# A decode step bound by its cache loads: K transposed in place, in a ring of eleven 16 KB units with a written-out plan of places

## The chip, the cores and the metric

The kernel runs on one core of a Trainium2 chip. A core has five engines that run their own instruction streams and meet at semaphores: PE (TensorE, matmuls), DVE (VectorE), ACT (ScalarE), POOL (GpSimd) and SP (SyncE, which here only issues transfers). Sixteen DMA engines move the data of all queues. The metric is the time of one execution in device microseconds (us); shown are the median of several runs and, for one profiled execution, its span from first to last instruction.

## What is computed

Two blocks work on the same four rows x (one token for each of four sequences, 1024 wide, bf16), and a gate mixes them.

```python
# A: attention of one new token against a cache; H = 32 heads, Dh = 128, Sk = 8192
q = (x @ wq).reshape(B, 1, H, Dh).transpose(0, 2, 1, 3)
scores = einsum("bhqd,bhkd->bhqk", q, k_cache) * Dh ** -0.5
p = softmax(scores)
o = einsum("bhqk,bhkd->bhqd", p, v_cache)
a = o.transpose(0, 2, 1, 3).reshape(B, 1, H * Dh) @ wo
# B: a gated MLP, F = 3584, added to x with a sigmoid weight r = x @ w_r
b = x + (silu(x @ w_gate) * (x @ w_up)) @ w_down * sigmoid(r)
# the mix
g = sigmoid((x * gate_w).sum(-1))
out = g * a + (1 - g) * b
```

Nearly all of the data is the two caches: each has 4 x 32 x 8192 x 128 bf16 values, 268 MB; the five weight matrices add some 39 MB. Every byte is used for one token only, so the work is a stream of some 576 MB through the core.

## The kernel before

**Tiles.** A *pair* is the K (or V) cache of four heads of one sequence: 8.39 MB, 64 KB in each of 128 partitions (`kv_view`). 128 heads make ND = 32 K pairs and 32 V pairs, called K0 to K31 and V0 to V31 here. A partition holds 256 consecutive positions of one head, 128 values each; 32 partitions make a head. A pair is worked in RD = 4 quarters of 16 KB per partition.

**The ring.** All large loads go through one SBUF tile of NS = 5 slots of 32 KB per partition. `load_pair` (line 189) takes the next two slots in turn. If they lie next to each other, one transfer brings the pair (line 196); where the ring wraps, and for V pairs called with `apart`, two transfers bring one half each (line 200). V29 to V31 are cut further by lines 568 to 573. `wd_piece` takes two slots for w_down, and `wo_block` puts four 8 KB blocks of wo into each of two slots. Every transfer is issued by SP in program order, and each waits, at SP, until what it overwrites has been read.

**A K pair** (`k_pair`, line 476 on for `spread`, 494 and 499 for the work). Scores need K with its 128 values on the partitions, and it arrives with positions there. DVE transposes blocks of 32 x 32 four-byte words: for each quarter two transposes (the two halves of the 128 values), eight in a pair, each from the ring into one of three buffers TB (`turned`, 8 KB per partition). PE then runs eight matmuls on each transposed half, with the heads' queries, spread out in Z, as stationary weights, and adds to the scores of the group in PSUM (S_ps). So a ring slot of K is free once DVE has read it, and a TB buffer once PE has.

**A V pair** (`v_pair`, line 579). PE takes V from the ring as it came: 64 matmuls with the probabilities PB as weights, into o_ps. A V slot is free once PE has read it. After every second V pair `sum_up` adds the four parts of o_ps: one step on ACT (L605), and three on DVE (L609), which wait in a list and are put into the next K pair after its third transpose; `finish` and `scaled` (L625, L634, L637) follow in the same K pair.

**Order.** Groups of GD = 8 K pairs share one softmax; after the eighth pair of a group its maximum, exponentials and their transposition run on DVE and ACT. PE, DVE and POOL run in the order of the program text. That order is: wq, w_gate, K0, K1, w_up, K2 to K7, then K8, V0, K9, V1 and so on (V follows K by LAG = 8), then w_down, V24 to V31, and the wo blocks, of which the first two are loaded ahead of V31.

Of the kernel before, what the change touches and what calls it, by code (L numbers as in the profile page):

```python
# [8 lines left out]
BF = mybir.dt.bfloat16  # L9
F32 = mybir.dt.float32  # L10
U32 = mybir.dt.uint32
# [101 lines left out]
def kernel(  # L113
# [15 lines left out]
    nc = tc.nc  # L129
    P = 128  # L130
    Bn, Sq, D = A_x.shape
    _, H, Sk, Dh = A_k_cache.shape
    F = B_w_gate.shape[1]
    DT = D // P
# [3 lines left out]
    CJ = 64  # L138
    JT = JR // CJ
    RD = 2 * JT  # L140
    GD = QP // RD
    GH = GD * NQ
    ND = Bn * H // NQ
# [5 lines left out]
    FR = 4  # L149
    FG = F // (P * FR)  # L150
    NB = 512
    NH = D // NB
    RING = JR * Dh
    NS = 5
    assert Sq == 1 and Dh == P and D % P == 0 and F % (P * FR) == 0
    assert H % GH == 0 and JR == 128 and RD * GD == QP and D % NB == 0
    scale = float(Dh) ** -0.5
# [3 lines left out]
    const = ctx.enter_context(tc.tile_pool(name="const", bufs=1))  # L161
# [7 lines left out]
    nc.at_finalize(drop_implied)  # L169
    nc.at_finalize(begin_early)  # L170

    ring = const.tile([P, NS, RING], BF, name="ring")
    turn = [0]


    TB = [const.tile([P, CJ * Dh // 2], BF, name=f"TB{i}") for i in range(3)]
    tb_turn = [0]

    def turned(rows, n, dtype=BF):
        t = TB[tb_turn[0] % 3]  # L180
        tb_turn[0] += 1
        return t[0:rows, 0:n] if dtype == BF else t[0:rows, 0:2 * n].bitcast(dtype)

    def slots(n):
        at = turn[0]
        turn[0] = (at + n) % NS
        return at

    flat = ring[:].rearrange("p s n -> p (s n)")

    def load_pair(src, n, apart=False):

        a = slots(2)
        if a + 1 < NS and not apart:
            lo = a * RING
            nc.sync.dma_start(out=flat[:, lo:lo + 2 * n], in_=src)
            return [flat[:, lo:lo + n], flat[:, lo + n:lo + 2 * n]]
        halves = [ring[:, a], ring[:, (a + 1) % NS]]
        for i, half in enumerate(halves):
            nc.sync.dma_start(out=half[:, 0:n], in_=src[:, i * n:(i + 1) * n])  # L200
        return halves


    S0 = scp.tile([P, 4, NB], F32, name="S_ps")
# [8 lines left out]
        return b[:, 0:n].rearrange("p (%s) -> p %s" % (" ".join(names), " ".join(names)), **dict(zip(names, shape)))  # L213

    N = H * Dh
    wq_at = load_pair(A_wq.rearrange("(c t) n -> c (t n)", t=DT), DT // 2 * N)
    NX = Bn + 2
    x6 = const.tile([NX, D], BF)
    nc.sync.dma_start(out=x6[0:Bn], in_=x2)
# [10 lines left out]
    n = 1  # L230
# [19 lines left out]
    for half in range(2):  # L250
        for e in range(2):
            nc.gpsimd.tensor_copy(out=R[:, 2 * half + e].rearrange("p (n j) -> p n j", n=4),
                                  in_=ident[:, 64 * half + e:64 * half + 64:2].unsqueeze(1).to_broadcast([P, 4, 32]))
# [57 lines left out]
    TW = DT // 2  # L311


    FI = FG * FR - 1
    FB = P * FI
    SX = 5
# [37 lines left out]

    def gu_piece(view, w_i):

        ws = load_pair(view.rearrange("(c t) f -> c (t f)", t=DT), TW * F)

        def cols(w, t, i):
            row = w[:, t * F:t * F + FB].rearrange("p (f m) -> p f m", m=FI)  # L360
            if i < FG - 1:
                return [(0, FR, row[:, :, FR * i:FR * i + FR])]
            return [(0, FR - 1, row[:, :, FR * i:FI]), (FR - 1, FR, w[:, t * F + FB:(t + 1) * F])]
        x_rows(o_ps[w_i], ws, FG, cols)
# [28 lines left out]
        nc.vector.tensor_tensor(out=hS[:], in0=hs_ps[0:72], in1=cS[:], op=ALU.mult)  # L393

    def wd_piece():
        a = slots(2)
        assert a + 1 < NS and (FI + SX) * D == 2 * RING
        w = flat[:, a * RING:(a + 2) * RING]
        at = FI * D
        nc.sync.dma_start(out=w[:, 0:at], in_=wdv)  # L400
        for u in range(2):
            nc.sync.dma_start(out=w[32 * u:32 * u + 12, at:at + SX * D], in_=wd_apart[u])
        nc.sync.dma_start(out=w[64:72, at:at + D], in_=wd_rest)
        parts = [(hT[:, i // FR, i % FR, :], w[:, i * D:(i + 1) * D]) for i in range(FI)]
        parts += [(hS[:, v, :], w[0:72, at + v * D:at + (v + 1) * D]) for v in range(SX)]
        for i, (lhsT, rows) in enumerate(parts):
            for n in range(NH):
                mm_acc(n, lhsT, rows[:, n * NB:(n + 1) * NB], start=(i == 0))
# [11 lines left out]
                                 rhs=OT[:, WB * g0 + k:WB * g1:WB, :], start=True, stop=True, skip_group_check=True)  # L420
        nc.vector.tensor_copy(out=LT[:, :, g0:g1, :], in_=lp)  # L421

    wo_home = {}

    def wo_block(g, r0=0, r1=FR, half=None):

        home, at = divmod(g, 4)
        if home not in wo_home:
            wo_home[home] = ring[:, slots(1)].rearrange("p (g r n) -> p g r n", g=4, r=FR)
        w = wo_home[home][:, at]  # L430
        if half is None:
            nc.sync.dma_start(out=w[:, r0:r1].rearrange("p r n -> p (r n)"),
                              in_=wov[:, g, r0:r1].rearrange("p r n -> p (r n)"))
        else:
            nc.sync.dma_start(out=w[:, r0, half * NB:(half + 1) * NB], in_=wov[:, g, r0, half * NB:(half + 1) * NB])

        def use():
            for r in range(r0, r1):
                for n in range(NH) if half is None else [half]:
                    mm_acc(n, LT[:, r, g, :], w[:, r, n * NB:(n + 1) * NB])  # L440
        return use
# [25 lines left out]
    def kv_view(cache, d):  # L467
        b, h0 = heads(d)
        return cache[b, h0:h0 + NQ].rearrange("h (r j) d -> (h r) (j d)", j=2 * JR)
# [8 lines left out]
    def k_pair(d):  # L478
        g, t = divmod(d, GD)
        Z = Zt[d % 2]  # L480
        if d == 0:
            spread(0)
        if t == 0:
            S_ps[g] = S0
        sps = S_ps[g]
        ks = load_pair(kv_view(A_k_cache, d), RING)
        for n in range(RD):
            kn = ks[n // JT].rearrange("p (c j h m) -> p c h j m", c=JT, h=2, m=Dh // 2)[:, n % JT]
            s = QP - 1 - (RD * t + n)
            for half in range(2):  # L490
                step = 2 * n + half
                flat_t = turned(P, CJ * Dh // 2)
                T = flat_t.rearrange("p (j i e) -> p j i e", j=CJ, e=2)
                nc.vector.transpose(out=flat_t.bitcast(U32).rearrange("p (j i) -> p j i", j=CJ), in_=kn[:, half].bitcast(U32))  # L494
                if step < 2 and ahead:
                    ahead.pop(0)()
                for e in range(2):
                    for z in range(4):
                        nc.tensor.matmul(sps[:, z, :], lhsT=Z[:, 2 * half + e, s:s + P], rhs=T[:, 16 * z:16 * z + 16, :, e],  # L499
                                         start=(t + n + half + e == 0),  # L500
                                         stop=(t == GD - 1 and n == RD - 1 and half + e == 2))
                if step == 2:
                    flush_sums()
                if step == RD and d + 1 < ND:
                    spread(d + 1)
                if step == RD:
                    flush()
                if step == RD + 2:
                    flush_late()
        if t == GD - 1:  # L510
            ahead.extend(softmax(g))
            while g > 0 and ahead:
                ahead.pop(0)()
# [45 lines left out]
    def v_pair(d):  # L559
        b, h0 = heads(d)  # L560
        g, t = divmod(d, GD)
        tv = t % GV
        row = NM * tv
        flush_sums()
        vv = kv_view(A_v_cache, d)
        if d < ND - 3:
            vs = load_pair(vv, RING, apart=d >= ND - GD + 2)
        else:
            vs = [ring[:, slots(1)] for _ in range(2)]
            for half, cuts in ((0, 1), (1, 2)) if d < ND - 1 else ((0, 2), (1, 4)):  # L570
                for c in range(cuts):
                    lo, hi = c * RING // cuts, (c + 1) * RING // cuts
                    nc.sync.dma_start(out=vs[half][:, lo:hi], in_=vv[:, half * RING + lo:half * RING + hi])
        for u in range(4 * RD):
            n, z = divmod(u, 4)
            vn = vs[n // JT]
            for w in range(4):
                j0 = CJ * (n % JT) + 16 * z + 4 * w
                nc.tensor.matmul(o_ps[w // 2][row:row + NM, w % 2, :],  # L579
                                 lhsT=PB[:, RD * (d % NW) + n, z].rearrange("p w s j -> p (w s j)"),  # L580
                                 rhs=vn[:, j0 * Dh:(j0 + 4) * Dh], start=(u == 0), stop=(u == 4 * RD - 1),
                                 skip_group_check=True)
            if u == 1:
                flush()
            if u == 7:
                flush_late()
        if tv == GV - 1:
            sum_up(d, g, t, b, h0)

        if g == NG - 1:  # L590
            if t < 2:
                spread_p(d + NW)
            if t == 3:
                spread_p(d + NW - 1, 2)
        elif t == NW - 1:
            spread_p(d + 1, NW)
        elif t == GD - 1:
            if g + 1 < NG - 1:
                spread_p(d + 1, NW)
            else:  # L600
                spread_p(d + NW)
# [47 lines left out]
    order = []  # L649
# [69 lines left out]
```

## Time and profile before

| | before |
|---|---|
| time, median of 3 runs | 1342.75 us (1342.62 to 1343.24) |
| profiled execution, span | 1340.5 us |
| PE busy | 1067.9 us, 80% |
| DVE busy | 638.3 us, 48% |
| queue of the loads (q1) | 575.69 MB, 99.7% of 16 engines' span |
| mean rate | 430 GB/s |

The page tells each engine's busy time, then cuts the span into 40 equal slices, each with the busy share of every engine in tenths and the rate of the transfers. The costliest groups follow: source line, engine, operation, what it writes and reads, how often, busy time and the mean of one, and then how long the engine was idle just before such instructions and what ended that. A group's mean is the time from issue to end of one, and PE's matmuls overlap, so the distance from one to the next is shorter than that mean. Further answers of the trace give the waits by engine and line (total, number, longest), the timeline of single instructions, and the chain of work that ended last, where a row "DMA" runs from a transfer's issue to its landing, the time in the queue included.

### The profile page before, as it was taken

To read this page: it belongs to the slowest core of one execution; us is meant where nothing else is said; L and a number is where in the kernel's file an instruction comes from. 1 tells how busy PE (TensorE), PEld (TensorE's weight loads), DVE (VectorE), ACT (ScalarE), POOL (GpSimd) and SP (SyncE) were. 2 spreads that over 40 slices of the span, in tenths; PEclk is the share of its full clock that TensorE was granted. 3 is DMA by queue.
4 is the path that set the end of the run, shared out by engine and by line. 5 is a ranking of instruction groups with operands and counts; after the bars stand their busy time and mean duration, and the time that the engine had idled before them with its cause. 6 is when DMAs were issued, how large, how long until landed. Compare 5 with 4: busy or idle time off the path is not lost.

```text
span 1340.5 us, 6937 instructions
## 1 busy us (share of the span) xinstructions
PE 1067.9 (80%) x4654; PEld 141.3 (11%) x1422; DVE 638.3 (48%) x385; ACT 57.7 (4%) x58; POOL 66.6 (5%) x174
## 2 busy tenths in 40 slices
PE   2666878887778788777879778789697879889888
PEld 0101000001011010101001010101011011111111
DVE  2555988556544347554436256646145555100001
ACT  0000000100010000100010000100000000110000
POOL 2000000100010000100010000100001000100000
PEclk9787999898998998898989888899898889889889
DMA  9999999999999999999999999999999999999998
GB/s 415 433 436 435 437 436 424 438 430 430 435 437 426 439 431 428 433 438 431 434 433 433 436 433 438 419 434 431 438 433 441 426 423 435 438 425 430 429 425 348
DMA packets 15512, 576.14 MB, mean 430 GB/s; under 512 B 1740, under 2 KB 2004, under 8 KB 3170
## 3 DMA queue, kind: packets, MB, share of 16 engines
q1 hardware_dynamic: 15474, 575.69, 99.7%
q8 instruction: 24, 0.39, 0.1%
q14 instruction: 6, 0.05, 0.0%
q10 hardware_dynamic: 8, 0.00, 0.0%
HBM read 575.68 MB, written 0.01 MB: 429 GB/s over the span
## 4 chain that ended last, share of the span: by engine, by line
DMA 62%; DVE 22%; PE 13%; another core or an unknown queue 1%; issue 0%; ACT 0%; SPq 0%; DVEq 0%
DMA ring<-in_A_k_cache_dram 51%; DVE TB L494 20%; DMA ring<-in_A_v_cache_dram 9%; PE o_ps L579 8%; PE S_ps L499 2%; PE acc L287 2%; DVE OS L609 2%; DMA x<-in_gate_w_dram 2%; DVE mx L521 0%; PE o_ps L333 0%; PE S_ps L333 0%; PE led L625 0%; DVE PT L535 0%; ACT TB L530 0%
## 5 line engine op out<-in xcount | busy, mean ns | idle before, releaser
L494 DVE STREAM_TRANSPOSE TB<-ring 128x2048 uint32<-128x2048 uint32 x256 | 568.2, 2278 | 471.7 <-DMA ring<-in_A_k_cache_dram 463.9
L499 PE MATMUL S_ps<-TB,Z 128*128 128x512 bf16 x2048 | 531.5, 414 | 186.0 <-DVE TB L494 178.4
L579 PE MATMUL o_ps<-ring,PB 128*64 128x512 bf16 x2048 | 468.5, 392 | 44.9 <-DMA ring<-in_A_v_cache_dram 43.7
L499 PEld LDWEIGHTS <-Z 128*128 128x128 bf16 x512 | 53.0, 103 | 649.6 <-issue 649.6
L579 PEld LDWEIGHTS <-PB 128*64 128x64 bf16 x512 | 57.6, 112 | 447.8 <-issue 443.4
L617 DVE SCALAR_TENSOR_TENSOR OS<-o_ps,mE,OS 128x512 f32<-128x512 f32 x5 | 3.8, 751 | 134.9 <-ACT OS L615 134.9
L476 POOL COPY Z<-qa 32x4 bf16<-32x4 bf16 x128 | 25.6, 200 | 719.2 <-PE S_ps L499 693.2
L555 POOL COPY PB<-PT 32x1024 bf16<-32x1024 bf16 (+3 forms) x23 | 33.3, 1446 | 456.8 <-PE o_ps L579 350.7
L605 ACT ACTIVATE OS<-o_ps,mE 128x512 f32<-128x512 f32 x11 | 7.6, 687 | 673.6 <-PE o_ps L579 673.6
L553 ACT COPY PB<-PT 32x1024 bf16<-32x1024 bf16 (+3 forms) x21 | 30.3, 1443 | 22.3 <-PE o_ps L579 17.3
L609 DVE SCALAR_TENSOR_TENSOR OS<-o_ps,mE,OS 128x512 f32<-128x512 f32 x33 | 24.3, 737 | 1.5
L530 ACT ACTIVATE TB<-S_ps,mx 128x2048 bf16<-128x2048 f32 x4 | 7.9, 1967 | 321.9 <-DVE mx L527 321.9
L287 PE MATMUL acc<-ring,hT 128*4 128x512 bf16 x54 | 14.7, 444 | 5.4 <-ACT TB L530 5.4
L245 PE MATMUL S_ps<-identb,x 6*128 6x6 bf16 x8 | 0.6, 196 | 22.6 <-DMA x<-in_gate_w_dram 22.6
L333 PE MATMUL o_ps<-ring,xw 128*4 128x512 bf16 (+2 forms) x128 | 13.2, 499 | 4.8 <-DMA ring<-in_B_w_gate_dram 4.8
L287 PE MATMUL acc<-ring,LT 128*4 128x512 bf16 x64 | 14.7, 379 | 0.4 <-DVE LT L421 0.4
L625 PEld LDWEIGHTS o_ps<-selg,OS 128*128 128x128 f32 x88 | 11.5, 191 | 9.3 <-issue 8.8
L535 DVE STREAM_TRANSPOSE PT<-TB 128x2048 bf16<-128x2048 bf16 x4 | 9.2, 2312 | 6.4 <-ACT TB L530 6.4
L521 DVE TENSOR_REDUCE mx<-S_ps 128x1 f32<-128x2048 f32 x4 | 9.1, 2282 | 6.2 <-PE S_ps L499 6.2
L625 PE MATMUL o_ps<-selg,OS 128*128 128x8 f32 x88 | 10.5, 245 | 0.0
L637 DVE SCALAR_TENSOR_TENSOR OT<-led,sgb,rinv 128x8 bf16<-128x8 f32 x5 | 1.2, 237 | 18.2 <-PE led L625 18.2
L615 ACT ACTIVATE OS<-o_ps,mE 128x512 f32<-128x512 f32 x5 | 3.4, 687 | 147.9 <-PE o_ps L579 147.9
(83 smaller groups left out, 89.2 us busy)
## 6 DMA issues: line engine op xcount, KB each, us to landing
ring<-in_A_v_cache_dram SPq DMA_DIRECT2D x18, 4096.0 KB, 28.9
ring<-in_A_k_cache_dram SPq DMA_DIRECT2D x14, 4096.0 KB, 33.2
ring<-in_A_v_cache_dram SPq DMA_DIRECT2D x6, 2048.0 KB, 36.7
ring<-in_B_w_gate_dram SPq DMA_DIRECT2D x1, 7168.0 KB
ring<-in_B_w_up_dram SPq DMA_DIRECT2D x1, 7168.0 KB, 37.1
ring<-in_B_w_down_dram SPq DMA_DIRECT2D x1, 6912.0 KB
ring<-in_A_wo_dram SPq DMA_DIRECT2D x4, 1024.0 KB, 32.5
ring<-in_A_v_cache_dram SPq DMA_DIRECT2D x4, 1024.0 KB, 36.0
```

The lines of the kernel that those rows point to most:

```text
L287: nc.tensor.matmul(acc(n), lhsT=lhsT, rhs=rhs, start=start, stop=True, skip_group_check=True)
L333: nc.tensor.matmul(ps[32 * k:32 * k + Bn, z, :].rearrange("p (f r) -> p f r", r=FR)[:, :, lo:hi], lhsT=xT[TW * half + t], rhs=rhs, start=( ...
L476: nc.gpsimd.tensor_copy(out=Z[at, :, QP - 1 + QP * q], in_=qa[at, :, h0 + q, b])
L494: nc.vector.transpose(out=flat_t.bitcast(U32).rearrange("p (j i) -> p j i", j=CJ), in_=kn[:, half].bitcast(U32))
L499: nc.tensor.matmul(sps[:, z, :], lhsT=Z[:, 2 * half + e, s:s + P], rhs=T[:, 16 * z:16 * z + 16, :, e], start=(t + n + half + e == 0), stop ...
L521: nc.vector.tensor_reduce(out=mx[:, 0:1], in_=sps[:].rearrange("p z n -> p (z n)"), axis=AX.X, op=ALU.max)
L535: nc.vector.transpose(out=PT[:].rearrange("p j i -> p (j i)"), in_=PTs)
L553: nc.scalar.copy(out=Bv[at, :, :, q, :], in_=Pv[at])
L555: nc.gpsimd.tensor_copy(out=Bv[at, :, :, q, :], in_=Pv[at])
L579: nc.tensor.matmul(o_ps[w // 2][row:row + NM, w % 2, :], lhsT=PB[:, RD * (d % NW) + n, z].rearrange("p w s j -> p (w s j)"), rhs=vn[:, j0 ...
L609: nc.vector.scalar_tensor_tensor(out=OS[:], in0=o_ps[w // 2][:, w % 2, :], scalar=mE[:, w:w + 1], in1=OS[:], op0=ALU.mult, op1=ALU.add)
L625: nc.tensor.matmul(oT, lhsT=OS[:, q * Dh:(q + 1) * Dh], rhs=selg[:, q].rearrange("p t s -> p (t s)"), start=(q == 0), stop=(q == 3), skip_ ...
```

## The change

K is transposed in place: input and output of the DVE transpose are the same elements of the ring, so that the TB buffers no longer carry K. They shrink from three of 8 KB to two of 4 KB, and the ring grows from 160 to 176 KB per partition: NU = 11 units of UN = 16 KB. A pair takes four units. Instead of taking turns, each load takes its place from a list, `plan`, of 68 entries in load order: the first unit, and whether the pair's quarters are worked upward or downward. A pair at unit 9 takes 9, 10, 0, 1, in two transfers. `wo_places` lists where the eight wo blocks go, in steps of 8 KB. V26 to V29 come in one transfer each; V30 in one half and two quarters, V31 in two and four parts (`cuts`).

The K matmuls read the transposed words where they lie: for 16 positions 32 elements with step 2 each, in place of 512 elements with step 2 in one run.

```diff
-    NS = 5
+    UN = RING // 2
+    NU = 11
-    ring = const.tile([P, NS, RING], BF, name="ring")
-    TB = [const.tile([P, CJ * Dh // 2], BF, name=f"TB{i}") for i in range(3)]
+    flat = const.tile([P, NU * UN], BF, name="ring")
+    UP, DOWN = False, True
+    plan = iter([
+        (4, UP), (0, UP), (4, UP), (0, DOWN), (7, UP), (3, UP), (7, UP), (1, UP), (5, DOWN), (0, DOWN), (7, UP), (1, UP),
+        (5, UP), (9, UP), (2, UP), (7, UP), (1, UP), (5, UP), (0, DOWN), (7, UP), (1, UP), (5, DOWN), (0, DOWN), (7, UP),
+        (1, UP), (5, DOWN), (0, DOWN), (7, UP), (3, UP), (7, UP), (1, UP), (5, DOWN), (0, DOWN), (7, UP), (1, UP), (5, DOWN),
+        (0, DOWN), (7, UP), (3, UP), (7, UP), (1, UP), (5, DOWN), (0, DOWN), (7, UP), (1, UP), (5, DOWN), (0, DOWN), (7, UP),
+        (2, UP), (7, UP), (0, UP), (5, UP), (9, UP), (2, UP), (7, UP), (0, UP), (5, UP), (9, UP),
+        (3, UP), (7, UP), (1, UP), (5, DOWN), (0, DOWN), (7, UP), (2, UP), (6, UP), (0, UP), (4, UP)])
+    wo_places = [20, 21, 16, 17, 18, 19, 0, 1]
+    TB = [const.tile([P, 4 * NB], BF, name=f"TB{i}") for i in range(2)]
-    def load_pair(src, n, apart=False):
-        a = slots(2)
-        if a + 1 < NS and not apart:
-            lo = a * RING
+    def load_pair(src, n, cuts=(1, 1)):
+        place, down = next(plan)
+        lo = place * UN
+        at = [lo, lo + n] if place + 4 <= NU else [lo, 0]
+        halves = [flat[:, x:x + n] for x in at]
+        if cuts == (1, 1) and at[1]:
             nc.sync.dma_start(out=flat[:, lo:lo + 2 * n], in_=src)
+        else:
+            for i, half in enumerate(halves):
+                step = n // cuts[i]
+                for x in range(0, n, step):
+                    nc.sync.dma_start(out=half[:, x:x + step], in_=src[:, i * n + x:i * n + x + step])
+        return halves, list(range(RD))[::-1] if down else list(range(RD))
...
-        ks = load_pair(kv_view(A_k_cache, d), RING)
-        for n in range(RD):
-            kn = ks[n // JT].rearrange("p (c j h m) -> p c h j m", c=JT, h=2, m=Dh // 2)[:, n % JT]
+        ks, order = load_pair(kv_view(A_k_cache, d), RING)
+        for k, n in enumerate(order):
+            unit = ks[n // JT][:, (n % JT) * UN:(n % JT + 1) * UN]
+            kn = unit.bitcast(U32).rearrange("p (j h i) -> p h j i", j=CJ, h=2)
+            T = unit.rearrange("p (j h i e) -> p h j i e", j=CJ, h=2, e=2)
-                flat_t = turned(P, CJ * Dh // 2)
-                T = flat_t.rearrange("p (j i e) -> p j i e", j=CJ, e=2)
-                nc.vector.transpose(out=flat_t.bitcast(U32).rearrange("p (j i) -> p j i", j=CJ), in_=kn[:, half].bitcast(U32))
+                nc.vector.transpose(out=kn[:, half], in_=kn[:, half])
-                        nc.tensor.matmul(sps[:, z, :], lhsT=Z[:, 2 * half + e, s:s + P], rhs=T[:, 16 * z:16 * z + 16, :, e],
+                        nc.tensor.matmul(sps[:, z, :], lhsT=Z[:, 2 * half + e, s:s + P], rhs=T[:, half, 16 * z:16 * z + 16, :, e],
...
-        if d < ND - 3:
-            vs = load_pair(vv, RING, apart=d >= ND - GD + 2)
-        else:
-            vs = [ring[:, slots(1)] for _ in range(2)]
-            for half, cuts in ((0, 1), (1, 2)) if d < ND - 1 else ((0, 2), (1, 4)):
+        vs, order = load_pair(vv, RING, {ND - 2: (1, 2), ND - 1: (2, 4)}.get(d, (1, 1)))
         for u in range(4 * RD):
-            n, z = divmod(u, 4)
+            n, z = order[u // 4], u % 4
```

The number of transposes, matmuls and bytes is the same. With all work of a K quarter done in the ring, a ring place of K is overwritten only after PE's matmuls on it.

More of the change, by code (lines that the diff above doesn't have):

```diff
@@ L170 @@
     nc.at_finalize(begin_early)
-    ring = const.tile([P, NS, RING], BF, name="ring")
-    turn = [0]
-    TB = [const.tile([P, CJ * Dh // 2], BF, name=f"TB{i}") for i in range(3)]
+    flat = const.tile([P, NU * UN], BF, name="ring")
[7 more added lines that the diff above has]
+        (3, UP), (7, UP), (1, UP), (5, DOWN), (0, DOWN), (7, UP), (2, UP), (6, UP), (0, UP), (4, UP)])
@@ L177 @@
+    wo_places = [20, 21, 16, 17, 18, 19, 0, 1]
+    TB = [const.tile([P, 4 * NB], BF, name=f"TB{i}") for i in range(2)]
     tb_turn = [0]
     def turned(rows, n, dtype=BF):
-        t = TB[tb_turn[0] % 3]
+        t = TB[tb_turn[0] % 2]
         tb_turn[0] += 1
         return t[0:rows, 0:n] if dtype == BF else t[0:rows, 0:2 * n].bitcast(dtype)
[L184 to L189, printed above, removed]
-    def load_pair(src, n, apart=False):
-        a = slots(2)
-        if a + 1 < NS and not apart:
-            lo = a * RING
[L196 to L201, printed above, removed]
+    def load_pair(src, n, cuts=(1, 1)):
+        place, down = next(plan)
+        lo = place * UN
+        at = [lo, lo + n] if place + 4 <= NU else [lo, 0]
+        assert at[1] or (n == RING and lo + n == NU * UN and not down)
+        halves = [flat[:, x:x + n] for x in at]
+        if cuts == (1, 1) and at[1]:
+            nc.sync.dma_start(out=flat[:, lo:lo + 2 * n], in_=src)
+        else:
[4 more added lines that the diff above has]
+        return halves, list(range(RD))[::-1] if down else list(range(RD))
@@ L215 @@
     N = H * Dh
-    wq_at = load_pair(A_wq.rearrange("(c t) n -> c (t n)", t=DT), DT // 2 * N)
+    wq_at, _ = load_pair(A_wq.rearrange("(c t) n -> c (t n)", t=DT), DT // 2 * N)
     NX = Bn + 2
@@ L355, in gu_piece @@
     def gu_piece(view, w_i):
-        ws = load_pair(view.rearrange("(c t) f -> c (t f)", t=DT), TW * F)
+        ws, _ = load_pair(view.rearrange("(c t) f -> c (t f)", t=DT), TW * F)
         def cols(w, t, i):
@@ L395, in wd_piece @@
     def wd_piece():
-        a = slots(2)
-        assert a + 1 < NS and (FI + SX) * D == 2 * RING
-        w = flat[:, a * RING:(a + 2) * RING]
+        lo = next(plan)[0] * UN
+        assert (FI + SX) * D == 2 * RING and lo + 2 * RING <= NU * UN
+        w = flat[:, lo:lo + 2 * RING]
         at = FI * D
@@ L421, in o_rows @@
         nc.vector.tensor_copy(out=LT[:, :, g0:g1, :], in_=lp)
-    wo_home = {}
     def wo_block(g, r0=0, r1=FR, half=None):
[L427 to L430, printed above, removed]
+        at = wo_places[g] * FR * D
+        w = flat[:, at:at + FR * D].rearrange("p (r n) -> p r n", r=FR)
         if half is None:
@@ L485, in k_pair @@
         sps = S_ps[g]
-        ks = load_pair(kv_view(A_k_cache, d), RING)
-        for n in range(RD):
-            kn = ks[n // JT].rearrange("p (c j h m) -> p c h j m", c=JT, h=2, m=Dh // 2)[:, n % JT]
+        ks, order = load_pair(kv_view(A_k_cache, d), RING)
[3 more added lines that the diff above has]
+            T = unit.rearrange("p (j h i e) -> p h j i e", j=CJ, h=2, e=2)
             s = QP - 1 - (RD * t + n)
             for half in range(2):
-                step = 2 * n + half
-                flat_t = turned(P, CJ * Dh // 2)
-                T = flat_t.rearrange("p (j i e) -> p j i e", j=CJ, e=2)
-                nc.vector.transpose(out=flat_t.bitcast(U32).rearrange("p (j i) -> p j i", j=CJ), in_=kn[:, half].bitcast(U32))
+                step = 2 * k + half
+                nc.vector.transpose(out=kn[:, half], in_=kn[:, half])
                 if step < 2 and ahead:
@@ L498, in k_pair @@
                     for z in range(4):
-                        nc.tensor.matmul(sps[:, z, :], lhsT=Z[:, 2 * half + e, s:s + P], rhs=T[:, 16 * z:16 * z + 16, :, e],
-                                         start=(t + n + half + e == 0),
-                                         stop=(t == GD - 1 and n == RD - 1 and half + e == 2))
+                        nc.tensor.matmul(sps[:, z, :], lhsT=Z[:, 2 * half + e, s:s + P], rhs=T[:, half, 16 * z:16 * z + 16, :, e],
+                                         start=(t + k + half + e == 0),
+                                         stop=(t == GD - 1 and k == RD - 1 and half + e == 2))
                 if step == 2:
@@ L565, in v_pair @@
         vv = kv_view(A_v_cache, d)
-        if d < ND - 3:
-            vs = load_pair(vv, RING, apart=d >= ND - GD + 2)
-        else:
-            vs = [ring[:, slots(1)] for _ in range(2)]
-            for half, cuts in ((0, 1), (1, 2)) if d < ND - 1 else ((0, 2), (1, 4)):
-                for c in range(cuts):
-                    lo, hi = c * RING // cuts, (c + 1) * RING // cuts
-                    nc.sync.dma_start(out=vs[half][:, lo:hi], in_=vv[:, half * RING + lo:half * RING + hi])
+        vs, order = load_pair(vv, RING, {ND - 2: (1, 2), ND - 1: (2, 4)}.get(d, (1, 1)))
         for u in range(4 * RD):
-            n, z = divmod(u, 4)
+            n, z = order[u // 4], u % 4
             vn = vs[n // JT]
```

## The prediction

> **What bounds the kernel now.** I read the page's slices and queues first, because they say whether the stream of loads ever stops; then the costliest groups, the waits of SP's own queue, and last the timeline and the chain around single K pairs. From the page:
>
> ```profile
> DMA  9999999999999999999999999999999999999998
> GB/s 415 433 436 435 437 436 424 438 430 430 435 437 426 439 431 428 433 438 431 434 433 433 436 433 438 419 434 431 438 433 441 426 423 435 438 425 430 429 425 348
> ...
> q1 hardware_dynamic: 15474, 575.69, 99.7%
> ...
> L494 DVE STREAM_TRANSPOSE TB<-ring 128x2048 uint32<-128x2048 uint32 x256 | 568.2, 2278 | 471.7 <-DMA ring<-in_A_k_cache_dram 463.9
> L499 PE MATMUL S_ps<-TB,Z 128*128 128x512 bf16 x2048 | 531.5, 414 | 186.0 <-DVE TB L494 178.4
> L579 PE MATMUL o_ps<-ring,PB 128*64 128x512 bf16 x2048 | 468.5, 392 | 44.9 <-DMA ring<-in_A_v_cache_dram 43.7
> ```
>
> The one queue that carries the caches has work in all 40 slices: 575.69 MB at about 432 GB/s is the whole span. DVE and PE wait for K, PE for V. The kernel can get faster only if the bytes move faster, and gets slower as soon as the queue runs empty. How far is it from empty? The waits of SP's queue, which issues the loads:
>
> ```profile
> SPq L196 <- DVE TB L494: 458.6, 25, 28.8
> SPq L196 <- PE o_ps L579: 370.3, 19, 27.3
> ```
>
> A load is issued when the ring place it overwrites has been read: a K place by the DVE transposes (L494), a V place by PE (L579). A K pair between sums, then one that holds them (timeline, then the chain):
>
> ```profile
> 270.23 17.66 DVE L494 STREAM_TRANSPOSE TB<-ring 128x2048 uint32<-128x2048 uint32 x8 [15.63 <-DMA ring<-in_A_k_cache_dram]
> ...
> 279.15 0.33 SPq L196 DMA_DIRECT2D ring<-in_A_k_cache_dram  x1
> ...
> 287.94 1.96 PE L499 MATMUL S_ps<-TB,Z 128*128 128x512 bf16 x8 [0.23 <-DVE TB L494]
> ...
> 289.97 0.95 POOL L476 COPY Z<-qa 32x4 bf16<-32x4 bf16 x4 [32.34 <-PE S_ps L499]
> ```
>
> ```profile
> 434.03 29.79 DMA ring<-in_A_k_cache_dram
> ...
> 463.91 6.70 DVE TB L494 x3
> 470.61 0.64 DVE OS L609
> ...
> 472.13 0.75 DVE OS L609
> 472.88 8.80 DVE TB L494 x4
> ...
> 481.80 2.22 DVE TB L494
> ...
> 484.06 1.96 PE S_ps L499 x8
> ```
>
> The pair that landed at 270.14 (issued 245.86, 24.28 to landing) is transposed in eight steps of 2.21 us; half of its ring place was free at 279.15, and PE had finished its last eight matmuls by 289.97 (POOL's copy waits for just that). So from landing to the end of PE's reading: 19.83 us. With the three sums of L609 inside, 463.82 to 486.0: 22.2 us; in the pair that landed at 308.83, where a reciprocal is added, PE ends at 331.43: 22.6 us.
>
> What does a load cost? Streaming, the chain has K landings at 581.43 (544.25 + 37.18) and 620.13 (590.44 + 29.69): 38.70 us for a K and a V pair, 19.35 each. Into an empty queue there is one row, the first load of the program, equally large:
>
> ```profile
> ring<-in_A_wq_dram SPq DMA_DIRECT2D x1, 21.9
> ```
>
> **The change part by part.**
>
> *Fewer, larger transfers.* The page counts 32 transfers of 4096 KB (14 K, 18 V) and 6 of 2048 KB; of the new plan's pairs only K9, V20 and K31 wrap, and only V30 and V31 are cut: 7 and 4. In the packet records a 64 KB packet takes 2425 ns, two of 32 KB 2435, four of 16 KB 2515. 25 transfers of 128 packets less make 1600 pairs of packets by 9.6 ns over 16 engines: 0.96 us. V29's second half saves (256 x 629 - 64 x 2425) ns / 16 = 0.36 us. Together -1.3 us, all on the path, since the queue is the path.
>
> *Transposing in place.* 256 transposes stay, 128x64x32 with a strided output in place of a dense one, and the matmuls read runs of 32 with step 2 in place of one run of 512. No row has an in-place one. The nearest, PT (L535, 2312 ns, dense, 2-byte) and L494 itself (2278 ns, 2.21 apart), are 1.5% apart; I take 2.21. Nothing excludes a cheaper one; the dearer side is bounded loosely by a tenth (2.43). DVE no longer waits for a TB buffer (7.7 us of waits in all): worth nothing, because the eight steps already run back to back in 17.66 us. The matmuls keep 1.96 us a step, under DVE's 2.21, with 0.25 us of cover.
>
> *A K place is now held until PE has read it*, not until DVE has: 2.0 us later for every K pair. Most issues can bear it. In the plan's regular stretch (K at 7, V at 1, K at 5 downward, V at 0 downward) a K load needs half of the K pair two transfers back: free 4 x 2.21 + 2.1 = 10.9 us after that pair's landing (13.2 with sums). A V load needs three quarters of the V pair two back, which PE starts at 19.9 and reads in 13.93: free at 30.3, wanted at 38. The queue then holds work for 19.0 us after a landing (19.35 less the 0.35 us from last byte to semaphore), so 5 to 8 us are spare.
>
> *Five issues have no such room.* Going through the 68 places in load order, five loads overwrite the *last-read* quarter of the K pair two transfers back, so need all of it: up (places 7 to 10) after K0 (4 to 7); K12 (7 to 10) after K11 (5 to 8 read upward); K17 after K16, K22 after K21 and K27 after K26 (7 to 10 after 7 to 10). Between them lies one transfer of 19.35 us; the pair takes 19.83 us. The queue empties every time. SP waits, the next V issue queued behind in order (its own place comes free 10 us later, so it loses nothing), and DVE and PE then wait for the late K pair. Each costs read-out + lone load - two streamed loads: 19.83 + 21.9 - 38.70 = 3.0 us for K0, K11, K21 (no sums: V pairs before them are even or absent), 22.2 + 21.9 - 38.7 = 5.4 for K16 and 22.6 + 21.9 - 38.7 = 5.8 for K26, which follow V7 and V17. Sum 9.0 + 11.2 = 20.2 us. If restarting cost nothing (19.35 for 21.9), 0.5, 3.0 and 3.4: 7.9 us. I take 21.9, the same size into an empty queue. The Trainium skill's page "DMA: Bandwidth & Descriptors" (Anatomy of one DMA) gives a fixed cost of some 2.0 us per transfer, mostly completion, next to bytes over 436 GB/s: as an estimate 21.2 us alone, and 16.7 us for the five together; no run here shows that figure, and its fit is for another issuing path. It speaks against letting the queue run dry as the wq row does.
>
> *Levelling.* In the semaphore records the sixteen engines finish one transfer 1.6 us apart at 60 us and 4.8 at the end: engine after engine loses about 1.4 us now and then and never regains it. An empty queue waits for the slowest, so each stretch between the five spells can lose its own 1.4 instead of sharing three: 0 to +4.4 us; I take 1.0, since spells also hide such losses.
>
> *V26 to V29 whole, the tail.* V29 now starts on PE only when all of it has landed. From that landing PE owes V29 13.9, V30 13.9 + 1.8 (L625), o_rows and wo block 0 2.6, V31 13.9 and, from 1323.8 to its end at 1337.45, the other wo blocks with finish, 13.6: 59.8 us, against 59.7 from V29's last landing (1277.7) to PE's end before. So PE has no idle time left there, where it had 3.9 us before 1287.6; any wait adds. I take 0.3, between 0 and 1. The ring of eleven units itself gives no time; wo blocks in fixed places overwrite pairs long read.
>
> Sum: -1.3 + 20.2 + 1.0 + 0.3 = +20.2 us. The profiled execution has a span of 1340.5 us, 2.2 under the median of 1342.75; the span becomes 1360.7 and the time about 1363.0.
>
> **The rivals.**
> *Dry spells nearly free.* The queue empties, but a restart costs only what is missing: 7.9 - 1.3 + 0.3 = +6.9, 1350 us. For it: the wq load was the program's first, colder than any later one (its first packets took 3.2 us, later ones 2.4). Against it: one landing and one issue lie in each spell anyway.
> *In-place transposes dearer.* Strided writes into lines that PE reads next to them could take 2.43 us: five spells x 8 x 0.22 = +8.8, 1372 us; above 2.5 us the K-only start would go dry too, over 1376. Nothing in the profile has this form, and DVE's input already is strided the same way.
> *Not slower.* In-place transposes at 1.8 us or less: read-out 16.6 us, so that even a restart is covered in three spells; or sums moved by waits out of the pair. Then -1.3 + 0.3, 1341.8 us, or 2 to 3 us less if the engines end level. The deciding point is a transpose of 1.83 us, (19.83 - 3.0 - 2.2) / 8; every 2048-column row of DVE lies at 2.28 or above. That the bytes move faster otherwise is excluded by the packet times, 27 bytes per ns whatever the size.
>
> **How the numbers follow.** As forecast 0.62 (1356 to 1369: restart 20.6 to 21.9 us, levelling 0 to 4.4); spells nearly free 0.17; transposes dearer 0.13; not slower 0.08, of which 0.03 is below 1340. The range takes in the first two and the tenth on the transposes: 1350 to 1373. Within 0.2% (2.7 us), about what this kernel's runs can tell from no change, lies 0.05; slower 0.92; faster 0.03.
>
> **What would show it.** Right: five waits of SP's K issues on PE's S_ps matmuls of 20 to 23 us after a landing, each with a K landing 41 to 45 us after the K landing two before in place of 38.7; the busy share of the queue falling to about 98%; SP's waits naming PE alone, no longer DVE; transposes still at 2.21 us apart. Wrong: a full queue at K12, K17, K22 and K27; a transpose below 1.9 or above 2.4 us; K12 issued before PE has read all of K11.

## The result

The changed kernel takes 1368.2 us (median of 4 runs, 1367.17 to 1369.29) against 1342.99 us before (1342.62 to 1343.41): a ratio of 1.0188, 95% interval 1.0175 to 1.0200, some 25 us slower. The profiled execution has a span of 1367.4 us, 26.9 more than the one of before.

From the page of the changed kernel, the lines that answer to those shown of before:

```profile
DMA  9989999999899999799999999999899999999998
GB/s 430 428 370 438 440 437 424 427 434 428 380 430 429 447 428 437 334 439 430 429 428 434 399 428 429 428 433 430 355 439 430 429 428 429 436 438 435 430 416 339
...
q1 hardware_dynamic: 13458, 575.69, 97.9%
...
L497 DVE STREAM_TRANSPOSE ring<-ring 128x2048 uint32<-128x2048 uint32 x256 | 567.9, 2278 | 494.7 <-DMA ring<-in_A_k_cache_dram 494.7
L502 PE MATMUL S_ps<-ring,Z 128*128 128x512 bf16 x2048 | 528.4, 413 | 239.9 <-DVE ring L497 231.1
L575 PE MATMUL o_ps<-ring,PB 128*64 128x512 bf16 x2048 | 459.4, 386 | 30.2 <-DMA ring<-in_A_v_cache_dram 29.0
```

The rate stands at its old 430 GB/s in all slices but five (370, 380, 334, 399, 355) and the last, which was low before too, and the queue's share of the span falls from 99.7% to 97.9%. The compute rows have not moved: a transpose in place takes 2278 ns, as out of place, and a matmul on the strided words 413 ns against 414. DVE and PE only wait longer for K. Where SP's queue waited for DVE before it overwrote a K place, it now waits for PE; the three costliest rows of its waits:

```profile
SPq L202 <- PE S_ps L502: 661.2, 30, 37.7
SPq L202 <- PE o_ps L575: 426.6, 26, 25.2
SPq L207 <- PE S_ps L502: 48.2, 4, 18.0
```

Two of the five slices closely, in the chain: first K11 (landed 353.11) and K12, then K16 (landed 551.79) and K17, with the sums inside.

```profile
353.13 17.68 DVE ring L497 x8
...
370.85 1.91 PE S_ps L502 x8
...
372.77 23.10 DMA ring<-in_A_k_cache_dram
```

```profile
551.82 6.70 DVE ring L497 x3
558.51 0.64 DVE OS L605
...
563.06 5.31 PE S_ps L502 x16
568.37 0.79 PE o_ps L621 x8
569.16 5.23 PE S_ps L502 x24
...
574.41 21.98 DMA ring<-in_A_k_cache_dram
```

DVE's steps follow on the landing, PE's last step follows on DVE, the issue of the next K load follows on PE, and that load is alone: 22 to 23 us from issue to landing, where a load in the middle of the stream comes 19.35 us after the one before it. The read-out, from the landing to the end of PE's reading, takes 19.7 and 22.6 us, longer than the one V transfer in between. From the end of that transfer to the late issue the queue has no work; such a stretch is called a spell below.

The semaphore records tell when the last of the sixteen DMA engines finished each load, and what the mean of the sixteen is. Against the same load of before (us):

| load | last engine before | after | its lateness grows by | mean lateness grows by |
|---|---|---|---|---|
| w_up (after K0) | 95.71 | 99.00 | 3.2 | 4.3 |
| K2 | 115.06 | 119.78 | 1.4 | 0.0 |
| K8 | 231.34 | 236.95 | 1.0 | 0.6 |
| K12 (after K11) | 386.30 | 395.88 | 4.1 | 4.1 |
| K17 (after K16) | 581.43 | 596.39 | 5.9 | 7.6 |
| V10 | 639.62 | 655.54 | 1.0 | -0.1 |
| K22 (after K21) | 775.16 | 793.73 | 2.8 | 3.7 |
| K23 | 813.87 | 833.94 | 1.3 | 0.1 |
| K27 (after K26) | 968.84 | 994.47 | 5.6 | 6.5 |
| V23 | 1161.24 | 1187.96 | 1.3 | 0.0 |
| V29 | 1277.72 | 1304.07 | in all 26.35 | in all 26.22 |

The five loads named in advance make 21.6 us at the last engine and 26.2 at the mean. All else lies within a few tenths per load and goes slightly the other way, 1.3 us in all at the last engine and 0.6 at the mean. (V23 is loaded after w_down, not before it as the order above has it.)

### The profile page after: what moved, and what is told of

Read it like the earlier page. It is cut to its first block, busy times and chain, and to the rows that moved or that the text cites. A ratio compares the mean times of both kernels' runs of the same rounds, so it can differ in the third digit from the quotient of the medians.

```text
span 1367.4 us, 6888 instructions
## 1 busy us (share of the span) xinstructions
PE 1055.9 (77%) x4654; PEld 141.7 (10%) x1422; DVE 638.0 (47%) x385; ACT 57.5 (4%) x58; POOL 66.3 (5%) x174
## 3 DMA queue, kind: packets, MB, share of 16 engines
q1 hardware_dynamic: 13458, 575.69, 97.9%
## 4 chain that ended last, share of the span: by engine, by line
DMA 59%; PE 22%; DVE 18%; issue 0%; ACT 0%; SPq 0%; DVEq 0%
DMA ring<-in_A_k_cache_dram 50%; DVE ring L497 16%; PE S_ps L502 11%; PE o_ps L575 8%; DMA ring<-in_A_v_cache_dram 6%; DMA ring<-in_B_w_gate_dram 3%; PE acc L294 2%; DVE OS L605 2%; PE o_ps L340 1%; PE led L621 0%; DVE mx L524 0%; DVE PT L538 0%; ACT TB L533 0%; PE o_ps L621 0%; DVE OS L613 0%
## 5 line engine op out<-in xcount | busy, mean ns | idle before, releaser
L497 DVE STREAM_TRANSPOSE ring<-ring 128x2048 uint32<-128x2048 uint32 x256 | 567.9, 2278 | 494.7 <-DMA ring<-in_A_k_cache_dram 494.7
L502 PE MATMUL S_ps<-ring,Z 128*128 128x512 bf16 x2048 | 528.4, 413 | 239.9 <-DVE ring L497 231.1
L575 PE MATMUL o_ps<-ring,PB 128*64 128x512 bf16 x2048 | 459.4, 386 | 30.2 <-DMA ring<-in_A_v_cache_dram 29.0
L556 ACT COPY PB<-PT 32x1024 bf16<-32x1024 bf16 (+3 forms) x21 | 30.1, 1434 | 21.7 <-PE o_ps L575 16.7
L252 PE MATMUL S_ps<-identb,x 6*128 6x6 bf16 x8 | 0.6, 197 | 22.2 <-DMA x<-in_gate_w_dram 22.2
## 6 DMA issues: line engine op xcount, KB each, us to landing
ring<-in_B_w_up_dram SPq DMA_DIRECT2D x1, 7168.0 KB, 19.9
```

What stands on the lines that cost most here:

```text
L497: nc.vector.transpose(out=kn[:, half], in_=kn[:, half])
L556: nc.scalar.copy(out=Bv[at, :, :, q, :], in_=Pv[at])
L575: nc.tensor.matmul(o_ps[w // 2][row:row + NM, w % 2, :], lhsT=PB[:, RD * (d % NW) + n, z].rearrange("p w s j -> p (w s j)"), rhs=vn[:, j0 ...
```

## The experiments

Two theories stood. The first: the loss is the five empty spells, set by the time that the whole K pair two loads back takes to be read out. The rival: transposing in place, or holding K until PE has read it, costs something at every pair, and the five slices are its sign only.

**The plan freed of the five waits.** Another 23 entries of the list; no load needs the last-read quarter of a K pair two loads back.

```diff
-        (4, UP), (0, UP), (4, UP), (0, DOWN), (7, UP), ...
-        (5, UP), (9, UP), (2, UP), (7, UP), (1, UP), (5, UP), (0, DOWN), (7, UP), (1, UP), (5, DOWN), (0, DOWN), (7, UP),
-        (1, UP), (5, DOWN), (0, DOWN), (7, UP), (3, UP), (7, UP), (1, UP), (5, DOWN), (0, DOWN), (7, UP), (1, UP), (5, DOWN),
...
+        (4, UP), (0, UP), (4, DOWN), (0, DOWN), (7, UP), ...
+        (5, UP), (9, UP), (2, UP), (7, UP), (1, UP), (5, DOWN), (0, DOWN), (7, UP), (1, UP), (5, DOWN), (0, DOWN), (7, UP),
+        (1, UP), (5, DOWN), (0, DOWN), (7, UP), (1, UP), (5, DOWN), (0, DOWN), (7, UP), (1, UP), (5, UP), (0, UP), (4, DOWN),
+        (0, DOWN), (7, DOWN), (3, UP), (9, UP), (2, UP), (6, UP), (0, UP), (4, DOWN), (0, DOWN), (7, DOWN), (3, UP), (9, UP),
+        (2, UP), (6, UP), (0, DOWN), (5, UP), (9, UP), (2, UP), (6, UP), (0, UP), (5, UP), (9, UP), (3, UP), (7, UP),
...
```

> The changed kernel with 23 of the 68 places or directions changed, so that no load needs the last-read quarter of the K pair two transfers back; everything else is as it was. Theory (the dry spells are the loss): the five K landings that came 2.7 to 5.9 us late (21.6 us together) are on time, and the engines' spread is no longer levelled at them (another 4 to 5 us): 1368.2 - 26 = 1342, between 1340.5 and 1344, with the queue's share back at 99.5% or more. Rival (transposing in place, or holding K until PE has read it, costs by itself at every pair): the time stays above 1347.

It took 1345.15 us (1343.65 to 1349.69), ratio 1.0022, 1.0013 to 1.0031. Three of its eleven runs lie at 1347.6 us or above, which no trace here explains. The page of this run:

```profile
q1 hardware_dynamic: 13746, 575.69, 99.5%
```

All but 2 of the 25 us are gone with the waits, while every pair is still transposed in place and held until PE has read it: the rival falls. The expectation was missed by 1.2 us, though. This plan is tight at other places: the mean engine loses 0.5 us at K6 and 0.7 at K20, which wait for three quarters of a K pair, and 1.0 at V26, issued 16.7 us after V24's landing. Waiting for three quarters is not the whole reason: K8 and K28 of this run do so too and lose 0.1 and 0.2.

**One word of the plan.**

```diff
-        (5, UP), (9, UP), (2, UP), (7, UP), (1, UP), (5, UP), (0, DOWN), ...
+        (5, UP), (9, UP), (2, UP), (7, UP), (1, UP), (5, DOWN), (0, DOWN), ...
```

> The changed kernel with one word changed: K11 is worked downward instead of upward, so that K12's place is half free 9 us earlier. Theory: the spell at K12 (4.07 us at the landing) goes, the four others stay: 1364, between 1362.5 and 1365.5 as the engines are levelled one time less. Rival (the backlog is short anyway and the next load is late in its place): 1367 to 1368.

It took 1364.32 us (1363.08 to 1365.29; ratio 1.0159, 1.0145 to 1.0173), 3.9 us less than the changed kernel. K12 comes in time, the spells at w_up, K17, K22 and K27 stay (2.9, 5.1, 3.0 and 5.9 us at the last engine). The price of one spell is what its place says; it isn't handed on to the next.

**In place in the old ring.**

```diff
+            unit = ks[n // JT][:, (n % JT) * UN:(n % JT + 1) * UN]
+            kn = unit.bitcast(U32).rearrange("p (j h i) -> p h j i", j=CJ, h=2)
+            T = unit.rearrange("p (j h i e) -> p h j i e", j=CJ, h=2, e=2)
-                nc.vector.transpose(out=flat_t.bitcast(U32).rearrange("p (j i) -> p j i", j=CJ), in_=kn[:, half].bitcast(U32))
+                nc.vector.transpose(out=kn[:, half], in_=kn[:, half])
```

> The kernel before with K transposed in place in its old ring of five 32 KB slots, nothing else. A K slot is then held 2.0 us longer, until PE has read it. Theory: the tightest issue before, at 245.86, came 24.3 us ahead of its landing, that is 4.9 us ahead of a streamed load's 19.35; a lone load needs 2.6 of these, so 2.4 us are spare, and 2.0 longer just fits: 1343, between 1342.3 and 1345, and transposes still 2.21 us apart. Rival (in place costs by itself): 8 x 0.1 us or more in each pair and SP's issues late all over, 1347 or more.

It took 1344.48 us (1343.24 to 1345.08). The interval of the ratio (1.0008, 0.9999 to 1.0018) still includes 1, but the median is 1.5 us above before and seven of the ten runs lie above the slowest of the 21 before, so a small loss is likely. From the page and the timeline of this run:

```profile
L495 DVE STREAM_TRANSPOSE ring<-ring 128x2048 uint32<-128x2048 uint32 x256 | 568.1, 2278 | 472.0 <-DMA ring<-in_A_k_cache_dram 472.0
...
248.01 0.33 SPq L197 DMA_DIRECT2D ring<-in_A_k_cache_dram  x1
```

The transposes keep their price, so transposing in place is not what costs the 25 us. What is lost fits the longer hold of the slot, and the tight place is where it was thought to be: the K load issued at 245.86 before now goes out at 248.01, and the mean engine loses 0.7 us there. Another 0.4 us goes at K29; in all V29 lands 1.9 us later at the mean engine and 2.2 at the last.

**More of the same spells.** K12 to K27 all in places 7 to 10, V3 to V18 in 0 to 3 and 3 to 6 in turn.

```diff
-        (5, UP), ..., (5, UP), (0, DOWN), (7, UP), (1, UP), (5, DOWN), (0, DOWN), (7, UP),
-        (1, UP), (5, DOWN), (0, DOWN), (7, UP), (3, UP), (7, UP), (1, UP), (5, DOWN), ...
+        (5, UP), ..., (5, UP), (0, DOWN), (7, UP), (3, UP), (7, UP), (0, DOWN), (7, UP),
+        (3, UP), (7, UP), (0, DOWN), (7, UP), (3, UP), (7, UP), (0, DOWN), (7, UP), ...
```

> The changed kernel with K12 to K27 all in places 7 to 10, worked upward, and V3 to V18 in 0 to 3 downward and 3 to 6 upward in turn: each of these K loads needs all of the K pair before it. Theory: each makes a dry spell, of 2.7 to 4.1 us after a pair without sums and 5.5 to 5.9 after one with: with K0's 3.2 they are 17 spells, 8 x 5.7 + 8 x 3.3 + 3.2 = 75 us in place of 21.6: 1421, between 1412 and 1427. Rival (the loss at K17, K22 and K27 belongs to something else at those times, such as the group's softmax or an instruction fetch): about 1368, up to 1380.

It took 1418.03 us in its one run, 75.0 above before. The queue's share falls to 95.0%:

```profile
q1 hardware_dynamic: 13458, 575.69, 95.0%
```

Seventeen spells are there, one for each whole wait. At the mean engine those after a pair without sums cost 2.6 to 4.5 us, those after one with sums 5.1 to 6.6. The spells alternate in size with the sums of every second V pair, wherever they lie in the softmax group.

**The plan kept, the load cut.** Seven loads come as two halves, the free one first.

```diff
+    split = {4: 1, 9: 0, 11: 1, 19: 1, 29: 0, 39: 0, 49: 0}
+    turn = iter(range(68))
...
+        first = split.get(next(turn))
...
+        if first is not None:
+            for i in (first, 1 - first):
+                nc.sync.dma_start(out=halves[i], in_=src[:, i * n:(i + 1) * n])
-        if cuts == (1, 1) and at[1]:
+        elif cuts == (1, 1) and at[1]:
```

> The changed kernel with its plan untouched; seven of the 68 loads (w_up, K6, K8, K12, K17, K22, K27) come as two transfers of one half each, the half whose place is free first going first. Theory (a whole pair waits for its last quarter, and the queue is empty meanwhile): the first half is issued at once and gives the queue 9.7 us more to live on, so that the second, free 19.8 to 22.6 us after the landing, comes in time: no spell, 1368.2 - 26 = 1342 plus up to 2 as in the run with the freed plan, between 1341 and 1345. Rival (the places themselves are late, however the load is cut): 1360 or more.

It took 1342.73 us (1342.45 to 1345.14) against 1342.9, ratio 1.0001, 0.9992 to 1.0010. The windows around K12, K17, K22 and K27, of the changed kernel and of this one (columns: window, its length, busy time and number of instructions of PE, weight loads, DVE, ACT and POOL, granted clock, share of the DMA engines, GB/s):

```profile
340.00:420.00 80.00, 61.04 (x260) 7.69 (x71) 37.61 (x20) 4.38 (x3) 5.31 (x10) 0.89 0.95 407
540.00:620.00 80.00, 59.67 (x250) 7.43 (x68) 38.03 (x21) 4.38 (x3) 6.09 (x14) 0.85 0.92 393
740.00:820.00 80.00, 61.76 (x263) 7.76 (x71) 37.62 (x20) 0.69 (x1) 1.55 (x8) 0.89 0.97 414
940.00:1020.00 80.00, 57.19 (x247) 7.43 (x69) 37.98 (x21) 0.69 (x1) 0.78 (x4) 0.89 0.92 394
```

```profile
340.00:420.00 80.00, 64.62 (x277) 8.06 (x75) 37.61 (x20) 4.38 (x3) 5.32 (x10) 0.91 1.01 434
540.00:620.00 80.00, 61.87 (x264) 7.86 (x72) 37.73 (x20) 2.27 (x2) 3.76 (x13) 0.89 1.00 433
740.00:820.00 80.00, 64.06 (x271) 8.09 (x74) 40.15 (x22) 0.69 (x1) 1.56 (x8) 0.91 1.00 432
940.00:1020.00 80.00, 62.06 (x269) 8.11 (x75) 39.30 (x22) 4.38 (x3) 5.31 (x10) 0.91 0.99 428
```

The places, the order and the work are the same; 393 to 414 GB/s become 428 to 434. That a load had to wait for *all four* of its units before any byte could move is the whole loss, to within the 1 us that the interval leaves. The waits themselves are not shorter: K17's first half went out at 555.9, its second only at 564.8, when PE was done with K16; but 9.7 us of data lay ahead of it.

**The sums out of two K pairs.** The pieces that run in K16 and K26 between transposes run after them.

```diff
-                if step == 2:
+                if step == 2 and d not in (16, 26):
                     flush_sums()
...
-                if step == RD:
+                if step == RD and d not in (16, 26):
                     flush()
-                if step == RD + 2:
+                if step == RD + 2 and d not in (16, 26):
                     flush_late()
```

> The changed kernel with the sums of V7 and V17 and what follows from them (finish, scaled) taken out of K16 and K26 and done after them, with the next V pair; nothing is left out. Theory (the read-out sets the spell): the spells at K17 and K27, 5.9 and 5.6 us, shrink to the 2.7 to 4.1 us of the others, 2 x 2.3 = 4.6 us less: 1363.6, between 1362 and 1366. Rival (those two spells are longer because of where they fall in the softmax group, or the sums only move the wait): 1367 or more.

It took 1363.21 us (1362.25 to 1363.57; ratio 1.0151, 1.0135 to 1.0167), 5.0 less than the changed kernel. In this run `finish` writes into the bank of o_ps to which V8 and V18 are adding, so the values of their heads change; the amount of work doesn't. K16's part of the chain, now without the sums:

```profile
550.70 17.68 DVE ring L497 x8
...
568.42 1.91 PE S_ps L502 x8
...
570.34 22.59 DMA ring<-in_A_k_cache_dram
```

The read-out takes 19.7 instead of 22.6 us, and the lateness at K17 grows by 3.6 instead of 5.9, at K27 by 2.7 instead of 5.6. The read-out shrinks by 3.0 us at K16 and 2.8 at K26, the two spells by 2.3 and 2.9: a spell follows the read-out to within 0.6 us.

## Why the prediction was right

*What bounds the kernel, and the sign.* Right. The stream of loads had no idle time, so a change in the ring could give next to nothing and lose as much as it let the queue run empty. The run with the split loads shows the other side of it: everything of the change but the spells is worth 0.2 us of gain, too little to tell from nothing.

*Five issues without room.* Right in each of the five, by name. The loads of w_up, K12, K17, K22 and K27 were issued 19.7, 19.7, 22.6, 19.7 and 22.5 us after the landing of the pair whose place they take; 19.8, 19.8, 22.2, 19.8 and 22.6 were forecast.

*The price of a spell.* For the five together 20.2 us were forecast and 21.6 measured at the last engine. Taking the wq load, 21.9 us alone, as the price of a restart was the better end: the five lone loads took 19.85 (w_up, 7.3 MB), 23.1, 22.0, 21.8 and 21.8 us. The rival of a nearly free restart (1350 us) would have needed 19.35; its 7.9 us for five spells is 7.5 by its own terms, which changes nothing. Three of the four lone pairs took 2.4 to 2.6 us more than a streamed one, K12 3.8. A 16 KB instruction fetch (381.9 us) lies in K12's load, and there one engine ends 1.5 us behind the mean; up to the landing of the mean engine all four pairs took 21.6 us. The fixed cost in the page "DMA: Bandwidth & Descriptors" (Anatomy of one DMA) of the Trainium skill, some 2.0 us, gave 21.2 us, an estimate. The 21.6 us at the mean engine, 2.2 more than a streamed load, come near it.

*Levelling: this is the term that was mis-sized.* 1.0 us was taken of a range of 0 to 4.4; the table has 1.4 (K2), 1.0 (V10), 1.3 (K23) and 1.3 (V23): 5.0 us, outside. The reason given for the low choice, that spells also hide such losses, was not seen. At each of these loads the mean engine loses nothing; at K2, V10 and K23 one engine falls behind the other fifteen, at V23 the three that were last fall back further. Each time an instruction fetch of 16 KB (queue q8 in the packet records) lies in the interval before the landing: at 103.4, 641.5, 817.5 and 1172.1 us. The run with one word changed loses 1.2, 1.3, 1.1 and 1.2 us at the same four loads, again each with a fetch. Before, one engine was already 1.6 us or more behind the first, and a fetch by another need not move the last landing. But about every third load has a fetch in its interval, and that the fetch is the cause was not tried. The simpler account is the last column of the table: counted at the mean engine the five spells cost 26.2 us, all there is (K8's 0.6 and the rest cancel). A spell should have been priced there: the engines that finish first wait longest.

*A sixth tight place* was not named: K8, 1.0 us at the last engine and 0.6 at the mean, waits for three quarters of K6 and was issued 15.3 us after its landing, 1.7 us before the first engine ran empty. "5 to 8 us are spare" was said of the regular stretch and not checked for the start, where K follows K. But the short lead does not by itself explain the 1.0 us. K6, issued 15.3 us after K4's landing and 1.6 us before the first engine ran empty, lost nothing, and in the three other runs with the same first twelve places K8 lost nothing at the last engine and 0.05 to 0.3 us at the mean. What made the difference stays open. Taken with those of the freed plan, ten such issues (K6 and K8 in five runs, 1.6 to 2.1 us before the first engine ran empty) lost 0.0 to 0.6 us at the mean engine. So a spare time is safe only if it is counted up to some 2.5 us before the queue is empty, not to its end.

*Transposing in place at the old price.* Right: 17.68 us for eight steps, 2278 ns each. The rival that it is dearer falls with this and with the run in the old ring.

*Transfers.* -1.3 us were forecast, with one wrong reading: 629 ns for a 16 KB packet is a mean that counts in the 24 instruction fetches of that size. The loads' own 16 KB packets took 615 ns, four of them 2460 in place of 2515, so V29's second half saves 0.14 us and not 0.36, and the sum is -1.1. With the spells gone by split loads the last wo block lands 0.35 us earlier than before (0.1 at the mean engine); the seven cuts add 7 x 128 x 9.6 ns / 16 = 0.5 us, so 0.6 was to be expected. The time itself can't tell such an amount. *Tail:* from the last landing to the end of the last copy on ACT it is 1.5 us (1363.5 to 1365.0) against 1.0 before (1337.04 to 1338.06): 0.5 us where 0.3 was forecast.

In sum: 26.35 us at V29's landing against a forecast of 19.9 (20.2 without the 0.3 of the tail); the difference is 4.0 of levelling, 1.0 of K8 and 1.4 of the spells, to within 0.1. The time, 1368.2 us, is 5.2 above the 1363.0 forecast. The misses of these three terms go the same way, so the number is not right by errors that cancel.

## What to carry to other kernels

In a kernel that lives on one saturated queue, a ring's plan is judged by one number for each load: how long before the queue runs empty its *last* place comes free, less the some 2.5 us that a restart took here. If one large transfer needs places that come free over 20 us, cut it where they do: here seven cuts in two were worth 25 us, and cost nothing that the time could tell. The work that decides is the read-out of the slowest reader, with everything that its engines do in between (here three sums of 0.7 us on DVE).

## What the runs showed of the hardware that was not expected

The sixteen DMA engines drift apart when the queue never empties: 1.6 us between first and last landing of a transfer at 60 us, 4.8 at 1160 us before. An empty spell brings them to 0.4 to 0.7 us again (w_up, K17, K22 and K27 here; at K12, with a fetch in the load, 1.9). Soon after a spell, at a load with a 16 KB instruction fetch in its interval, one engine falls back by some 1.0 to 1.4 us again (K2, V10 and K23); the two were seen together and not tried apart. A kernel that is bound by its slowest engine thus paid more for several short spells than the idle time of that engine at the spells tells: here 21.6 us at them and 5.0 us after them. In-place and strided forms were free: the transposes read and wrote the same words while PE read their neighbours, at the same 2.21 us a step.
